# A prepass with its four Q/K pairs first and its four V rounds behind them, and its staging moved into bytes of the loop's tiles

## The chip, the cores and the metric

The kernel runs on one core of a Trainium2 chip. The time is the device time of one execution in microseconds (us). Before the change it was 1764.0, 1775.37 and 1770.44 us in three runs, median 1770.44. The profile comes from one further execution of the same program, 1772.28 us, whose profiled span is 1770.6 us.

Engines are named as in the profile: PE is TensorE (matrix multiplications; PEld its loads of stationary operands), DVE is VectorE, ACT is ScalarE, POOL is GpSimd, SP is SyncE. SP and ACT issue nearly all DMAs; the queue of a DMA is named after its issuer (SPq, ACTq). A DMA that waits at the head of an engine's queue holds whatever that engine was to do next.

## What is computed

Two attentions of the same 2048 x 640 input are mixed by a gate per token. One is a local attention with 8 taps at a distance of two tokens (32 heads of 20). The other walks through 64 segments of 32 tokens and carries 8 memory rows from segment to segment (32 heads of 192):

```python
mem = mem0
for s in range(n_seg):                      # 64 segments, one after the other
    h = concat([mem, x[s * 32:(s + 1) * 32]])          # 40 rows
    q, k, v = h @ Wq, h @ Wk, h @ Wv                   # 640 -> 32 heads x 192
    p = softmax(where(mask, q @ k.T * scale, -1e9))
    o = (p @ v) @ Wo                                   # back to 640
    mem = o[:8]
    outs.append(o[8:])
a = concat(outs)
out = sigmoid(x @ gate_w) * a + (1 - sigmoid(x @ gate_w)) * b     # b: the local attention
```

A segment needs the memory of the one before, so the loop over segments can't be spread out. What depends on x alone can be computed ahead of it.

## The kernel before

The program has four stages.

**Part B** (`part_b`) is the local attention. On its way it prepares the other stages: `make_xT(b)` transposes 512 tokens of x at a time, POOL copies them into `xh_blk` (L184, L185), and SP stores that for the loop's segments (L186). POOL makes a second copy of each segment's last eight tokens, `zx_blk` (L190), which SP stores as well (L191, 160 KB each, four of them). Late in part B, SP loads all of that back as `zT` (640 KB, L320), and POOL makes a second layout of it, `zTi` (L321). `zT` has token `i` of segment `s` at column `s i`, `zTi` at column `i s`. Both are 128 x 2560 bf16. `load_early` issues the first weight slices once the first xh store has been issued, then 20 copies of Wo slices into a scratch in DRAM (`wscr`).

**The weights** are 80 slices of 128 x 1536 bf16 (384 KB): 20 each of Wq, Wk, Wv and 20 of Wo (12 `oa`, 8 `ob`). 14 of them are streamed anew in every segment through five buffers (`wst`); 66 stay resident. The resident ones are sorted in the order of their use (`use`, L374) and loaded on SP in four lots: 21 early ones in part B, 24 when part B ends (`load_late(0)`), 8 in the last Q/K pair (`load_late(1)`, N_MID), and 13 behind the prepass (`load_late(2)`, N_LAST), so those 13 stand ahead of the loop's own streaming on SP's queue.

**The prepass** (`prepass`) projects the last eight tokens of all 64 segments, 512 columns, with Wq, Wk and Wv. `project_qk(p)` is a pair: two groups of eight heads of Wq (p = 0, 1) or of Wk (p = 2, 3), 24 groups of five matmuls of 128 x 512, whose results ACT and DVE evict in turn (`evac`, L75 and L77) into a tile ZS of 128 x 64 x 192. ACT then stores ZS to `zpk_dram`, in two DMAs. `project_v(R)` is a V round: four steps of three groups of five matmuls, evicted into a tile ZV, which ACT stores with two DMAs for each step. All groups take their PSUM from one pool of eight banks. The order is pair 0, V 0, pair 1, V 1, pair 2, V 2, pair 3, V 3.

**The loop** (`part_a`) runs 64 segments in an order written out by hand for PE, ACT and DVE. Per segment it multiplies 32 columns (`hT`) with all of Wq and Wk (`m_qk`, L568), then Wv (`m_v`, L661) and Wo (`o_group`, L725). It reads the segment's part of `zpk_dram` (`load_z`, L543, and `load_vz`, L548; ACT's queue). Behind it, `part_z` computes the output rows of the last eight tokens of each segment.

The scheduler of the framework decides which PSUM bank a group gets and which semaphore a wait goes to; the order of the instructions within each engine follows the program above, except where `issue_after` ties an instruction to a DMA.

```python
for s0, s1 in ((0, 8), (8, nseg)):
    nc.scalar.dma_start(self.zpk_dram[s0:s1, :, z0:z0 + 192].rearrange("s p f -> p s f"), ZS[:, s0:s1, :])
```

Of the kernel before, what the change touches and what calls it, by code (L numbers as in the profile page):

```python
# [10 lines left out]
BF = mybir.dt.bfloat16  # L11
# [3 lines left out]
N_STREAM = 14  # L15
N_EARLY = 21
N_MID = 8
ZVB = 4
N_LAST = 13
WBUFS = 5  # L20
# [6 lines left out]
class _K:  # L27

    def __init__(self, ctx, tc, A_x, A_mem0, A_Wq, A_Wk, A_Wv, A_Wo, seg_len, B_wqkv, B_wo, gate_w, out):
        self.ctx, self.tc, self.nc = ctx, tc, tc.nc  # L30
        self.x2d = A_x.rearrange("b s d -> (b s) d")
        self.out2d = out.rearrange("b s d -> (b s) d")
        self.mem0 = A_mem0.rearrange("b m d -> (b m) d")
        self.Wq = A_Wq.rearrange("d h e -> d (h e)")
        self.Wk = A_Wk.rearrange("d h e -> d (h e)")
        self.Wv = A_Wv.rearrange("d h e -> d (h e)")
        self.Wo = A_Wo.rearrange("h e d -> (h e) d")
        self.wqkv, self.wo, self.gate_w = B_wqkv, B_wo, gate_w
# [12 lines left out]
        self.hTp = ctx.enter_context(tc.tile_pool(name="hTp", bufs=2))  # L51
        self.zctx = ExitStack()
        self._evac_i = 0
        self.evac_pat = _DEV.get("evac_pat", "aaad")
# [33 lines left out]
    def part_b(self):  # L88

        nc, tc, KC, S = self.nc, self.tc, self.KC, self.S  # L90
        NQ, HALO = 121, 14
        BQ = 4 * NQ
        scale_b = 20.0 ** (-0.5)
        self.bsc_dram = self.dram.tile([S, 640], BF, name="bsc_dram")
        self.zT_dram = self.dram.tile([128, KC, S // 32, 8], BF, name="zT_dram")
        self.oz_dram = self.dram.tile([S // 32, 128, 384], BF, name="oz_dram")
# [4 lines left out]
        with ExitStack() as ctx:  # L101
# [56 lines left out]
            def make_xT(b):  # L158
                t0 = 512 * b
                for kc in range(KC):  # L160
                    ps = bank(BF, "ps_xT")
# [26 lines left out]
                self.first_store = self.first_store or xh_store.ins  # L188
                zx = blkp.tile([128, KC, 16, 8], BF, name="zx_blk")
                nc.gpsimd.tensor_copy(zx[:].rearrange("p c s i -> p s c i"), xv[:, :, :, 24:32])  # L190
                nc.sync.dma_start(self.zT_dram[:, :, 16 * b:16 * b + 16, :].rearrange("p c s i -> p c (s i)"),  # L191
                                  zx[:].rearrange("p c s i -> p c (s i)"))

# [7 lines left out]
            def make_v(b):  # L201
                nq, nu, c0 = shape_of(b)
                nk = nq + 7
                for u in range(nu):
                    V = wk.tile([128, 652], BF, name=f"bV{u}")
                    nc.gpsimd.memset(V[:, 640:652], 0.0)
                    k0 = c0 + 242 * (u // 2) + u % 2
# [81 lines left out]
            nc.scalar.preload_act_table_set("natural_log_exp_and_others")  # L289
            zp = self.zctx.enter_context(tc.tile_pool(name="pre_z", bufs=1, side="right"))  # L290
            self.zT = zp.tile([128, KC, S // 4], BF, name="zT")
            self.zTi = zp.tile([128, KC, S // 4], BF, name="zTi")
            sel_ones = wp.tile([128, 160], BF, name="sel_ones")
            steps = [(b, g) for b in range((S + BQ - 1) // BQ) for g in range(8)]
            self.first_store = None
# [6 lines left out]
            for i, (b, g) in enumerate(steps):  # L302
# [11 lines left out]
                if (b, g) == (1, 4):  # L314
                    self.build_sel(self.const, sel_ones[:])
                    self.hT0 = self.load_seg(0)
                    for kc in range(KC):
                        nc.sync.dma_start(self.hT0[:, kc, 0:8], self.mem0[:, kc * 128:(kc + 1) * 128].rearrange("m p -> p m"))
                if (b, g) == (S // 512 - 1, 2):
                    nc.sync.dma_start(self.zT[:], self.zT_dram[:].rearrange("p c s i -> p c (s i)"))  # L320
                    nc.gpsimd.tensor_copy(self.zTi[:].rearrange("p c (i s) -> p c i s", i=8),  # L321
                                          self.zT[:].rearrange("p c (s i) -> p c i s", i=8))
                if g == 6 and i + 8 < len(steps):
# [32 lines left out]
    def weights_setup(self):  # L356
# [13 lines left out]
        rest = [k for k in keys if k not in self.stream_keys]  # L370
        use = [g for p in range(4) for g in (("qqkk"[p], 2 * (p % 2)), ("qqkk"[p], 2 * (p % 2) + 1), ("v", p))]
        rest.sort(key=lambda k: use.index(k[:2]) if k[:2] in use else 99)
        n = (0, N_EARLY, len(rest) - N_MID - N_LAST, len(rest) - N_LAST, len(rest))
        self.early, *self.late = [rest[n[x]:n[x + 1]] for x in range(4)]  # L374
        self.wres = self.ctx.enter_context(tc.tile_pool(name="wres", bufs=1))
# [43 lines left out]
    def prepass(self):  # L419
# [6 lines left out]
        def project_qk(p, pool):  # L426
# [3 lines left out]
            if p == 3:  # L430
                self.load_late(1)
            for r in range(2):
# [12 lines left out]

        def project_v(R):
            sls = [self.get_slice(("v", R, kc)) for kc in range(KC)]
            for st in range(NZ // 128):
# [68 lines left out]
    def part_a(self):  # L517
# [4 lines left out]
        with ctx:  # L522
            pers = ctx.enter_context(tc.tile_pool(name="a_pers", bufs=1, reuse_waits="tile"))
            ZQ = pers.tile([128, 224 + 768 + 1152], BF, name="ZQ")
            Vz = ZQ[:, 224:608]
            QTa = ZQ[:, 992:2144].rearrange("p (b r c i) -> p b r c i", b=6, r=2, i=8)
            Es = [ZQ[:, 608 * h:608 * h + 224].rearrange("p (a f) -> p a f", a=2) for h in range(2)]
            zst = ZQ[:, 32:416]
            oTz = zst.rearrange("p (c q) -> p c q", q=8)
            whi = ZQ[:, 1376:1376 + 640]  # L530
            KV = pers.tile([128, 1536], BF, name="KV")
# [3 lines left out]
            a4 = pers.tile([128, 160], BF, name="a4")  # L535
            KTz = pers.tile([128, 12, 32], BF, name="KTz")

# [4 lines left out]
            def load_z(s):  # L542
                nc.scalar.dma_start(ZQ[:, 608:1376], self.zpk_dram[s, :, 384:1152])  # L543
                nc.gpsimd.tensor_copy(KTz[:].rearrange("p c (R i) -> p c R i", i=8),  # L544
                                      ZQ[:, 608:992].rearrange("p (R c i) -> p c R i", c=12, i=8))

# [342 lines left out]
def kernel(  # L889
# [57 lines left out]
```

## Time and profile before

| | us |
|---|---|
| median of three runs (lowest, highest) | 1770.44 (1764.0, 1775.37) |
| the profiled execution | 1772.28 |
| its span | 1770.6 |
| part B | 0 to 232.0 |
| prepass, first to last matmul | 232.03 to 389.3 |
| segment 0 of the loop | 389.3 to 428.6 |
| segment 1 | 428.6 to 448.8 |

Busy shares of the whole span: PE 95% (1675.4 us), ACT 49%, DVE 37%, POOL 4%. The DMA engines move 467.81 MB, 264 GB/s on average. In the slices of the page, each a fortieth of the span (44.3 us), the ones of part B and the prepass look like this (a digit is the busy share in tenths):

```profile
PE   6888999987999999999999999999999999999989
ACT  3766632223555555555555555555555555555550
DMA  5951176579999999899999989989989999998991
```

PE is near full from the fifth slice to the end but for the ninth and tenth, 354 to 443 us, where the prepass ends and the loop starts. ACT and DVE carry part B; in the loop PE does. An idle engine costs time only where another one waits for it, so what counts is PE's idle time, and the clock at which it runs.

### The profile page before, as it was taken

Reading aid. Unit: us, or ns where it says so; the run is one execution under the profiler, and the core shown is the slowest. Engines: PE = TensorE matmul, PEld = TensorE weight load, DVE = VectorE, ACT = ScalarE, POOL = GpSimd, SP = SyncE. Lnnn points to the kernel's source line nnn. Section 1 sums busy time; section 2 is a strip of 40 time slices with the busy share of each in tenths; the row PEclk is TensorE's granted clock in tenths of the full one; section 3 lists DMA queues with packets and bytes.
Section 4 is the critical chain, followed back from the end, with each engine's and each line's share of the span. In section 5 each row is a group of like instructions: output and inputs, shape, how many; then the busy total and the mean of one; then the engine's idle time right before and its main releaser. Section 6 shows DMA issues by size and latency. Waiting matters only on the chain.

```text
span 1770.6 us, 82392 instructions
## 1 busy us (share of the span) xinstructions
PE 1675.4 (95%) x36512; PEld 995.8 (56%) x36527; DVE 651.8 (37%) x2047; ACT 869.2 (49%) x2377; POOL 75.0 (4%) x151
## 2 busy tenths in 40 slices
PE   6888999987999999999999999999999999999989
PEld 3555544434565655556555555555555555555557
DVE  4565532322333333333333333333333333333330
ACT  3766632223555555555555555555555555555550
POOL 6011000000000000000000000000000000000000
PEclk9999999998999999999999999999999999999999
DMA  5951176579999999899999989989989999998991
GB/s 161 331 128 50 38 258 164 154 234 328 290 303 303 303 301 306 297 297 311 302 298 303 306 284 304 302 289 297 304 297 298 301 298 303 303 296 292 306 299 30
DMA packets 283480, 467.81 MB, mean 264 GB/s; under 512 B 97524, under 2 KB 158452, under 8 KB 283124
## 3 DMA queue, kind: packets, MB, share of 16 engines
q1 hardware_dynamic: 181400, 403.14, 68.9%
q10 hardware_dynamic: 101724, 59.41, 11.6%
q8 instruction: 285, 4.67, 1.1%
q14 instruction: 71, 0.58, 0.1%
HBM read 428.13 MB, written 42.20 MB: 266 GB/s over the span
## 4 chain that ended last, share of the span: by engine, by line
PE 83%; ACT 6%; DMA 6%; issue 3%; DVE 1%; ACTq 0%; SPq 0%; POOL 0%; DVEq 0%; POOLq 0%
PE ps_qk L568 25%; PE ps_v L661 13%; PE ps_wo L725 11%; PE ps_qkT L585 6%; PE ps_S L615 5%; PE ps_pre L438 5%; PE ps_oT L684 3%; PE ps_z L879 3%; PE ps_bqk L224 3%; ACT bP L247 2%; PE ps_pre L453 2%; ACT ZQ L806 2%; PE ps_bv L211 1%; PE ps_mem L735 1%; PE ps_S L624 1%
## 5 line engine op out<-in xcount | busy, mean ns | idle before, releaser
L577 ACT CAST KV<-ps_qk 128x384 bf16<-128x384 f32 x448 | 208.5, 480 | 333.0 <-PE ps_qk L568 185.0
L568 PEld LDWEIGHTS <-hT 128*32 128x32 bf16 x10240 | 247.7, 96 | 154.5 <-DVE hT L738 12.8
L568 PE MATMUL ps_qk<-wlate_k,hT 128*32 128x384 bf16 x4352 | 269.9, 329 | 1.2 <-issue 0.9
L592 DVE COPY ZQ<-ps_qkT 128x384 bf16<-128x384 bf16 x256 | 91.6, 358 | 390.0 <-PE ps_qkT L585 220.3
L568 PE MATMUL ps_qk<-wres_q,hT 128*32 128x384 bf16 x4096 | 227.4, 329 | 4.6 <-ACT ZV L75 3.8
L633 ACT ACTIVATE ZQ<-ps_S 32x224 bf16<-32x224 f32 x512 | 178.1, 348 | 44.3 <-PE ps_S L624 39.8
L725 PEld LDWEIGHTS <-KV 128*32 128x32 bf16 x6144 | 154.1, 96 | 67.7 <-issue 20.2
L661 PE MATMUL ps_v<-wlate_v,hT 128*32 128x384 bf16 x2816 | 160.6, 329 | 0.0
L568 PE MATMUL ps_qk<-wst,hT 128*32 128x384 bf16 x1792 | 153.9, 329 | 1.0 <-issue 1.0
L661 PEld LDWEIGHTS <-hT 128*32 128x32 bf16 x5120 | 113.4, 96 | 72.7 <-issue 10.0
L725 PE MATMUL ps_wo<-wlate_oa,KV 128*32 128x384 bf16 x2560 | 140.5, 327 | 2.9 <-issue 2.8
L615 PE MATMUL ps_S<-ZQ,KV 128*128 128x160 bf16 (+1 forms) x1024 | 136.9, 238 | 3.3 <-DMA ZQ<-zpk_dram 3.3
L585 PE MATMUL ps_qkT<-ident,KV 128*128 128x128 bf16 x1536 | 130.7, 221 | 0.4 <-issue 0.3
L725 PE MATMUL ps_wo<-wlate_ob,KV 128*32 128x256 bf16 x2688 | 123.6, 275 | 7.3 <-issue 7.3
L585 PEld LDWEIGHTS <-KV 128*128 128x128 bf16 x1536 | 89.4, 98 | 61.9 <-issue 40.9
L695 DVE CAST KV<-ps_oT 128x192 bf16<-128x192 f32 x256 | 79.4, 351 | 64.8 <-PE ps_oT L689 64.8
L615 PEld LDWEIGHTS <-KV 128*128 128x128 bf16 (+1 forms) x1024 | 59.1, 95 | 72.6 <-issue 45.3
L695 ACT CAST KV<-ps_oT 128x192 bf16<-128x192 f32 x256 | 69.6, 326 | 59.0 <-PE ps_oT L689 59.0
L544 POOL COPY KTz<-ZQ 128x384 bf16<-128x384 bf16 x64 | 32.6, 509 | 1492.1 <-DMA ZQ<-zpk_dram 850.6
L661 PE MATMUL ps_v<-wst,hT 128*32 128x384 bf16 x1024 | 87.1, 330 | 9.1 <-DMA wst<-in_A_Wv_dram 9.1
L738 DVE CAST hT<-ps_mem 128x24 bf16<-128x24 f32 x126 | 22.6, 179 | 197.4 <-PE ps_mem L735 197.4
L668 ACT CAST KV<-ps_v 128x384 bf16<-128x384 f32 x192 | 92.4, 481 | 3.1
(127 smaller groups left out, 2316.8 us busy)
## 6 DMA issues: line engine op xcount, KB each, us to landing
wst<-in_A_Wq_dram SPq DMA_DIRECT2D x260, 384.0 KB
wst<-in_A_Wv_dram SPq DMA_DIRECT2D x260, 384.0 KB
wst<-in_A_Wk_dram SPq DMA_DIRECT2D x195, 384.0 KB
wst<-wscr SPq DMA_DIRECT2D x192, 384.0 KB
ZQ<-zpk_dram ACTq DMA_DIRECT2D x64, 192.0 KB
zpk_dram<-ZS ACTq DMA_DIRECT2D x4, 2688.0 KB
wscr<-in_A_Wo_dram SPq DMA_DIRECT2D x20, 384.0 KB
wlate_k<-in_A_Wk_dram SPq DMA_DIRECT2D x17, 384.0 KB
```

Source lines behind the costliest of these rows:

```text
L224: nc.tensor.matmul(ps[:, 0:nn], lhsT=wqk[n][:, kc, 4 * g:4 * g + 4, :].rearrange("p h d -> p (h d)"), rhs=xT[:, kc, o0:o0 + nn], start=(kc ...
L438: nc.tensor.matmul(ps[:], lhsT=sls[r][kc][:, c0:c0 + 128], rhs=zT[:, kc, :], start=(kc == 0), stop=(kc == KC - 1))
L568: nc.tensor.matmul(pq[32 * j:32 * j + 32, 0:384], lhsT=hT[:, kc, :], rhs=sl[:, 384 * j:384 * j + 384], start=(kc == 0), stop=(kc == KC - 1 ...
L577: cp(sts[i], pqs[i][:, 0:384])
L585: nc.tensor.transpose(pT[:, t, :, :, :].rearrange("p j b i -> p (j b i)"), st[:, 128 * t:128 * t + 128], self.ident[:])
L592: nc.vector.tensor_copy(q_blocks(R)[:, 1:5, :, :].rearrange("p b c i -> p c b i"), pT.rearrange("p t j b i -> p (t j) b i"))
L615: nc.tensor.matmul(grid(h, par)[:, :, 0:80].rearrange("p j (b r i) -> p j b r i", r=2, i=8)[:, :, :, r, :], lhsT=KT[k0:k1, 12 * r + c:12 * ...
L633: nc.scalar.activation(E[ps], pSs[h][ps, :, 112 * j:112 * j + 112], ACT.Exp, scale=scale_a)
L661: nc.tensor.matmul(pvs[R][32 * j:32 * j + 32, 0:384], lhsT=hT[:, kc, :], rhs=sl[:, 384 * j:384 * j + 384], start=(kc == 0), stop=(kc == KC ...
L668: cp(V[R], pvs[R][:, 0:384])
L695: cps[j % 2](oTxs[2 * h + j // 2][:, 6 * (j % 2):6 * (j % 2) + 6, :], pos[j][:, 0:240].rearrange("p (c q) -> p c q", q=40)[:, :, 8:40])
L725: nc.tensor.matmul(pso[part][32 * jj:32 * jj + 32, 0:n], lhsT=oTxs[2 * (R // 2) + j // 2][:, 6 * (j % 2) + 3 * (R % 2) + t, :], rhs=o_weig ...
```

## The change

- The prepass runs the four Q/K pairs first, then the four V rounds. The weights are sorted and loaded in that order (q, k, v).
- There is one x^T of the last tokens, `zTi` in the layout `i s`, in a tile `TZ` of the constants. POOL writes it straight from the transposed x in `make_xT`, after the xh store is issued. `zx_blk`, the DRAM tensor `zT_dram`, its four stores, its load and the copy at L321 are gone. The pairs now multiply with `zTi` too, so their evictions read PSUM with the eight tokens of one segment 64 elements apart.
- Each ZS goes out in one DMA of 64 segments instead of two (8 and 56).
- ZV lies in the bytes of pair 2's ZS, and eight late slices (N_V) are loaded into the bytes of pair 3's, issued ahead of the V rounds. The lots are now 23 early, 27 at the end of part B, 4 in the last pair, 8 ahead of the V rounds and 4 (N_LAST) behind the prepass.
- In the loop, KV, KTz, Vz, the output staging and one E tile lie in the bytes of `TZ`; the rest of ZQ is a tile `ZB` that also holds `a4`.
- The selection masks (`build_sel`) are built in the last `make_xT` instead of at step (1, 4), and the memsets of V's padding go from POOL to DVE.

```diff
-N_EARLY = 21
-N_MID = 8
+N_EARLY = 23
+N_MID = 4
+N_V = 8
+N_LAST = 4
 ZVB = 4
-N_LAST = 13
...
+        self.TZ = self.const.tile([128, self.KC * self.S // 4], BF, name="TZ")
+        self.zTi = self.TZ[:].rearrange("p (c x) -> p c x", c=self.KC)
...
-                zx = blkp.tile([128, KC, 16, 8], BF, name="zx_blk")
-                nc.gpsimd.tensor_copy(zx[:].rearrange("p c s i -> p s c i"), xv[:, :, :, 24:32])
-                nc.sync.dma_start(self.zT_dram[:, :, 16 * b:16 * b + 16, :].rearrange("p c s i -> p c (s i)"),
-                                  zx[:].rearrange("p c s i -> p c (s i)"))
+                with tc.issue_after(xh_store.ins):
+                    nc.gpsimd.tensor_copy(zTi[:, :, :, 16 * b:16 * b + 16],
+                                          xv[:, :, :, 24:32].rearrange("p s c i -> p c i s"))
+                    if b == 3:
+                        self.build_sel(self.const, sel_ones[:])
...
-                    nc.gpsimd.memset(V[:, 640:652], 0.0)
+                    nc.vector.memset(V[:, 640:652], 0.0)
...
-                if (b, g) == (S // 512 - 1, 2):
-                    nc.sync.dma_start(self.zT[:], self.zT_dram[:].rearrange("p c s i -> p c (s i)"))
-                    nc.gpsimd.tensor_copy(self.zTi[:].rearrange("p c (i s) -> p c i s", i=8),
-                                          self.zT[:].rearrange("p c (s i) -> p c i s", i=8))
...
-        use = [g for p in range(4) for g in (("qqkk"[p], 2 * (p % 2)), ("qqkk"[p], 2 * (p % 2) + 1), ("v", p))]
+        use = [(m, R) for m in "qkv" for R in range(4)]
...
-                            nc.tensor.matmul(ps[:], lhsT=sls[r][kc][:, c0:c0 + 128], rhs=zT[:, kc, :],
+                            nc.tensor.matmul(ps[:], lhsT=sls[r][kc][:, c0:c0 + 128], rhs=zTi[:, kc, :],
...
-                        self.evac(ZS[:, :, zc:zc + 8], ps[:].rearrange("p (s i) -> p s i", i=8))
-            z0 = 768 + 192 * (1 - Rp) if m == "q" else 384 + 192 * Rp
-            for s0, s1 in ((0, 8), (8, nseg)):
-                nc.scalar.dma_start(self.zpk_dram[s0:s1, :, z0:z0 + 192].rearrange("s p f -> p s f"), ZS[:, s0:s1, :])
+                        self.evac(ZS[:, :, zc:zc + 8], ps[:].rearrange("p (i s) -> p s i", i=8))
+            nc.scalar.dma_start(self.zpk_dram[:, :, z0:z0 + 192].rearrange("s p f -> p s f"), ZS[:])
...
-        with tc.tile_pool(name="pre_zv", bufs=ZVB, side="right", reuse_waits="tile") as zvp, \
-                tc.tile_pool(name="pre_zs1", bufs=1, side="right", reuse_waits="tile") as zs1:
-            zT, zTi = self.zT, self.zTi
+        zTi = self.zTi
+        with tc.tile_pool(name="pre_zs1", bufs=1, side="right", reuse_waits="tile") as zs1:
             with tc.tile_pool(name="pre_zs0", bufs=1, reuse_waits="tile") as zs0:
                 project_qk(0, zs0)
-                project_v(0)
                 project_qk(1, zs1)
-                project_v(1)
                 project_qk(2, zs0)
-            project_v(2)
             project_qk(3, zs1)
-            project_v(3)
-        self.zctx.close()
+        vs = [[self.get_slice(("v", R, kc)) for kc in range(KC)] for R in range(4)]
+        self.load_late(2, "right")
+        with tc.tile_pool(name="pre_zv", bufs=ZVB, reuse_waits="tile") as zvp:
+            for R in range(4):
+                project_v(vs[R], R)
...
-            ZQ = pers.tile([128, 224 + 768 + 1152], BF, name="ZQ")
+            ZB = pers.tile([128, 1536 + 160], BF, name="ZB")
+            KV, ZA = self.TZ[:, 0:1536], self.TZ[:, 1920:2528]
...
-    k.load_late(2)
+    k.load_late(3)
```

More of the change, by code (lines that the diff above doesn't have):

```diff
@@ L51, in __init__ @@
         self.hTp = ctx.enter_context(tc.tile_pool(name="hTp", bufs=2))
-        self.zctx = ExitStack()
+        self.TZ = self.const.tile([128, self.KC * self.S // 4], BF, name="TZ")
+        self.zTi = self.TZ[:].rearrange("p (c x) -> p c x", c=self.KC)
         self._evac_i = 0
@@ L94, in part_b @@
         self.bsc_dram = self.dram.tile([S, 640], BF, name="bsc_dram")
-        self.zT_dram = self.dram.tile([128, KC, S // 32, 8], BF, name="zT_dram")
         self.oz_dram = self.dram.tile([S // 32, 128, 384], BF, name="oz_dram")
@@ L289, in part_b @@
             nc.scalar.preload_act_table_set("natural_log_exp_and_others")
-            zp = self.zctx.enter_context(tc.tile_pool(name="pre_z", bufs=1, side="right"))
-            self.zT = zp.tile([128, KC, S // 4], BF, name="zT")
-            self.zTi = zp.tile([128, KC, S // 4], BF, name="zTi")
+            steps = [(b, g) for b in range((S + BQ - 1) // BQ) for g in range(8)]
+            zTi = self.zTi.rearrange("p c (i s) -> p c i s", i=8)
             sel_ones = wp.tile([128, 160], BF, name="sel_ones")
-            steps = [(b, g) for b in range((S + BQ - 1) // BQ) for g in range(8)]
             self.first_store = None
@@ L314, in part_b @@
                 if (b, g) == (1, 4):
-                    self.build_sel(self.const, sel_ones[:])
                     self.hT0 = self.load_seg(0)
@@ L370, in weights_setup @@
         rest = [k for k in keys if k not in self.stream_keys]
-        use = [g for p in range(4) for g in (("qqkk"[p], 2 * (p % 2)), ("qqkk"[p], 2 * (p % 2) + 1), ("v", p))]
+        use = [(m, R) for m in "qkv" for R in range(4)]
         rest.sort(key=lambda k: use.index(k[:2]) if k[:2] in use else 99)
-        n = (0, N_EARLY, len(rest) - N_MID - N_LAST, len(rest) - N_LAST, len(rest))
-        self.early, *self.late = [rest[n[x]:n[x + 1]] for x in range(4)]
+        n = (0, N_EARLY, -N_MID - N_V - N_LAST, -N_V - N_LAST, -N_LAST, None)
+        self.early, *self.late = [rest[n[x]:n[x + 1]] for x in range(5)]
         self.wres = self.ctx.enter_context(tc.tile_pool(name="wres", bufs=1))
@@ L431, in project_qk @@
                 self.load_late(1)
+            z0 = 768 + 192 * (1 - Rp) if m == "q" else 384 + 192 * Rp
             for r in range(2):
@@ L437, in project_qk, with project_v @@
                         for kc in range(KC):
-                            nc.tensor.matmul(ps[:], lhsT=sls[r][kc][:, c0:c0 + 128], rhs=zT[:, kc, :],
+                            nc.tensor.matmul(ps[:], lhsT=sls[r][kc][:, c0:c0 + 128], rhs=zTi[:, kc, :],
                                              start=(kc == 0), stop=(kc == KC - 1))
                         zc = 96 * r + 8 * (4 * t + j)
-                        self.evac(ZS[:, :, zc:zc + 8], ps[:].rearrange("p (s i) -> p s i", i=8))
-            z0 = 768 + 192 * (1 - Rp) if m == "q" else 384 + 192 * Rp
-            for s0, s1 in ((0, 8), (8, nseg)):
-                nc.scalar.dma_start(self.zpk_dram[s0:s1, :, z0:z0 + 192].rearrange("s p f -> p s f"), ZS[:, s0:s1, :])
-        def project_v(R):
-            sls = [self.get_slice(("v", R, kc)) for kc in range(KC)]
+                        self.evac(ZS[:, :, zc:zc + 8], ps[:].rearrange("p (i s) -> p s i", i=8))
+            nc.scalar.dma_start(self.zpk_dram[:, :, z0:z0 + 192].rearrange("s p f -> p s f"), ZS[:])
+        def project_v(sls, R):
             for st in range(NZ // 128):
@@ L523, in part_a @@
             pers = ctx.enter_context(tc.tile_pool(name="a_pers", bufs=1, reuse_waits="tile"))
-            ZQ = pers.tile([128, 224 + 768 + 1152], BF, name="ZQ")
[L525 to L528, printed above, removed]
+            ZB = pers.tile([128, 1536 + 160], BF, name="ZB")
+            KV, ZA = self.TZ[:, 0:1536], self.TZ[:, 1920:2528]
+            Vz = ZA[:, 224:608]
+            QTa = ZB[:, 384:1536].rearrange("p (b r c i) -> p b r c i", b=6, r=2, i=8)
+            Es = [z[:, 0:224].rearrange("p (a f) -> p a f", a=2) for z in (ZA, ZB)]
+            zst = ZA[:, 32:416]
             oTz = zst.rearrange("p (c q) -> p c q", q=8)
-            whi = ZQ[:, 1376:1376 + 640]
-            KV = pers.tile([128, 1536], BF, name="KV")
+            whi = ZB[:, 768:768 + 640]
             KT = KV[:, 0:768].rearrange("p (c k) -> p c k", k=32)
@@ L534, in part_a @@
             oTxs = [v.rearrange("p (c q) -> p c q", q=32) for v in V]
-            a4 = pers.tile([128, 160], BF, name="a4")
-            KTz = pers.tile([128, 12, 32], BF, name="KTz")
+            a4 = ZB[:, 1536:1696]
+            KTz = self.TZ[:, 1536:1920].rearrange("p (c k) -> p c k", k=32)
             psm = ctx.enter_context(tc.tile_pool(name="psm", bufs=2, space=bass.MemoryType.PSUM, reuse_waits="tile"))
@@ L542, in load_z @@
             def load_z(s):
-                nc.scalar.dma_start(ZQ[:, 608:1376], self.zpk_dram[s, :, 384:1152])
+                nc.scalar.dma_start(ZB[:, 0:768], self.zpk_dram[s, :, 384:1152])
                 nc.gpsimd.tensor_copy(KTz[:].rearrange("p c (R i) -> p c R i", i=8),
-                                      ZQ[:, 608:992].rearrange("p (R c i) -> p c R i", c=12, i=8))
+                                      ZB[:, 0:384].rearrange("p (R c i) -> p c R i", c=12, i=8))
             def load_vz(s):
```

## The prediction

> **What bounds the kernel now.** I read the page first (TensorE busy 95% of the span, so only its stalls and clock can be won), then the busy times by stage, because the change reorders one stage, the prepass, and so moves what stands before and after it.
>
> ```profile
> core 0: us, PE busy (x) PEld busy (x) DVE busy (x) ACT busy (x) POOL busy (x), PEclk, DMA share, GB/s
> 0.00:232.00 232.00, 197.76 (x2724) 115.43 (x2725) 126.65 (x233) 139.46 (x249) 42.42 (x87) 0.96 0.46 136
> 271.00:389.30 118.30, 116.37 (x530) 52.59 (x538) 36.69 (x55) 29.71 (x54) 0.00 (x0) 1.00 0.62 173
> 389.30:428.60 39.30, 25.13 (x491) 14.39 (x490) 7.95 (x27) 11.79 (x34) 0.51 (x1) 0.83 0.95 323
> 428.60:448.80 20.20, 19.96 (x501) 12.04 (x502) 7.30 (x27) 10.60 (x32) 0.51 (x1) 1.00 0.93 301
> ```
> Columns: window, its length, busy us and count per engine, granted clock, DMA share, GB/s. Part B ends at 232.0. In the prepass TensorE is nearly full. Segment 0 takes 39.3 us where segment 1 takes 20.2: 19.1 us too many, at a clock of 0.83. That is nearly all there is to win. Its chain of waits (start, us, what):
>
> ```profile
> 388.78 3.79 DMA wst<-in_A_Wk_dram
> 392.57 0.09 ACT ZV L75
> ...
> 409.13 7.79 DMA wst<-in_A_Wv_dram
> ```
> and its instructions in order of time (start, us, engine, line, operation; in brackets the idle time before):
>
> ```profile
> 397.45 6.71 SPq L399 DMA_DIRECT2D wlate_oa<-wscr  x6
> ...
> 403.21 0.47 PE L615 MATMUL ps_S<-ZQ,KV 128*128 128x160 bf16 x4 [2.33 <-DMA ZQ<-zpk_dram]
> ...
> 404.20 4.40 SPq L399 DMA_DIRECT2D wlate_ob<-wscr  x7
> ...
> 404.81 1.50 PE L568 MATMUL ps_qk<-wres_q,hT 128*32 128x384 bf16 x16
> ...
> 416.96 0.51 PE L661 MATMUL ps_v<-wst,hT 128*32 128x384 bf16 x4 [7.42 <-DMA wst<-in_A_Wv_dram]
> ```
> Three stalls (3.79, 2.33, 7.42 us) and a small one (0.31): 13.85 us. The rest, 19.1 - 13.85 = 5.2, is slow clock: the 16 matmuls at 404.81 take 1.50 us, the same 16 at 399.38 took 0.82. The 7.42 us stall is a queue: 13 late slices stand ahead of one slice of Wv on SP. The first two come from ScalarE, which also issues the Z stores:
>
> ```profile
> L75 ACT CAST ZS<-ps_pre x48: 586/586/641, 233.3 to 375.4; 128x512 bf16<-128x512 f32 x48
> ...
>   DMA zpk_dram<-ZV: 25.9, 3
> ...
> 382.82 9.63 ACTq L460 DMA_DIRECT2D zpk_dram<-ZV  x4
> 392.55 1.56 ACT L75 CAST ZV<-ps_pre 128x512 bf16<-128x512 f32 x3 [9.22 <-DMA wst<-in_A_Wk_dram]
> ```
> After each pair's ZS store (landing 13.45 us after its issue) the next V stores hold ScalarE's queue 8.9 to 9.6 us, and evictions queue behind them. The last round has the loop behind it, not another pair: hence 3.79 at 389.
>
> **The change, part by part.** The profiled execution took 1772.28 us (span 1770.6); the median of three is 1770.44, 1.84 below it.
>
> *Matmuls of the prepass: the same.* Before, a pair's 120 matmuls end 25.9 us after they began (232.03 to 257.92), a V round's 60 take 12.95. Four of each are 155.4; the stage took 157.3 (232.03 to 389.32). So 1.9 us of stalls go, the largest 1.04 at 360.
>
> *Pairs back to back.* A group of five 128x512 matmuls takes 1.08 us; its eviction starts 0.42 us after the next group begins and lasts 0.59 (ScalarE) or 0.69 (VectorE), so a bank is free 1.1 us after its group's end. In the built program before, each of these groups takes a bank used six groups or more earlier. In the new one, four groups early in each of pairs 1, 2 and 3 wait for VectorE's eviction of the group 4, 3, 2 and 1 earlier. Distances 4 and 3 are covered (two groups are 2.16 us); distance 1 costs 1.1, distance 2 about 0.1: 3 x 1.2 = **+3.6 us**, at least 0 if the eviction drains ahead, at most 6. The 1.04 us stall at 360 left the clock at 1.00 (window 360 to 380), so I add nothing for it.
>
> *Strided eviction.* x^T lies with the segment inside, so 96 evictions read PSUM with a step of 64 elements. No row of before reads PSUM so. The nearest: VectorE's eviction that permutes runs of eight takes 0.36 us, as the contiguous one does; POOL's zTi copy, reading single elements, takes 4.83/2560 = 1.89 ns an element against 0.717/640 = 1.12 for runs of eight, factor 1.7. Two engines alternate, so each has 2.16 us an eviction; 0.69 x 1.7 = 1.17 fits, and only the three distance-1 waits grow, by 0.5 each. I take 0 (nearest engine and memory), range 0 to +1.5.
>
> [...]
>
> *V rounds.* The ScalarE block happens once, behind pair 3, not four times. In V0 its stores hold ScalarE until the ZS store has landed, and the next ones wait for DMA semaphores held by the first of eight late slices, issued only when ZS has landed (1.2 + 13.45 = 14.7 us after pair 3's end). Before, at 350.95, the same knot took until 360.54, 9.6 us, plus an eviction of 0.6: ScalarE is through at 24.9, where TensorE wants that bank 21 groups after pair 3, at 22.7: **+2.2 us** (0 to 4, with a clock drop at the upper end). V1 to V3 run free. Removing 1.9 and adding 3.6 + 2.2 makes the prepass **+3.9 us**.
>
> *Segment 0.* V3's evictions are no longer blocked: the first groups wait only for VectorE's last ones, 0.4 us; the Z loads are issued a round early, so the 2.33 goes; load_vz behind V3's stores costs up to 0.5. On SP four late slices stand ahead of the Wv slice, not 13. Before, the streamed slice ahead of them was issued 3.76 us after the first loop matmul (393.19 to 396.95) and 15 tiles landed in 20.0 us, 1.33 each (0.98 at the 402 GB/s of 410 to 420). That one, four and Wv's are six tiles, 5.9 to 8.0 us: landing 9.7 to 11.8 after the start, with up to 1.3 of latency on top, wanted at 10.5 (as in segment 1) plus the 0.9 just named: a stall of 0 to 1.5, taken 0.7. A stall of over 2 us costs 5.2/3 = 1.7 us of clock besides; I take a third of that. Segment 0: 20.2 + 0.4 + 0.5 + 0.7 + 0.6 = 22.4 against 39.3: **-16.9 us**. The nine late slices that left the loop's start are hidden under 104 us of pairs and 52 of V rounds (DMA share there 0.62); without that cover each costs 1.33.
>
> *Part B and other queues.* SP loses four zT stores and the 640 KB load; POOL loses the 4.83 us copy, its four 0.72 copies become strided (1.2 by the factor), and its 18 memsets of 0.1 go to VectorE (55% busy there). The masks are built at the last x^T block. The early loads start up to 4.5 us sooner (POOL waits that long for the band before the zx copy that SP follows), but are two more slices, of 28.4/21 = 1.35 each (29.62 to 58). TensorE waits here for ScalarE and VectorE, so I take **0**, from -2 to +2. The zT path ended in a 9.9 us POOL wait that nothing else waited for.
>
> *The loop.* The built program's instructions and waits in a steady segment are the same ones; only addresses differ. 0, with a tail: 0.05 us a segment is 3.2 us.
>
> Sum: +3.9 - 16.9 + 0 = -13.0: 1759.3 against the profiled execution, and 1770.44 - 13.0 = 1757.4 against the median, said as **1758 us**.
>
> **The rivals.**
> 1. *Everything hidden.* Semaphore waits and late loads land in time: the 3.6, 2.2 and segment 0's 2.2 shrink to 2 in all: -1.9 - 19.1 + 2 = -19, 1751 us. For: the DMA queues have slack in the pairs. Against: a distance-1 wait can't be hidden. Chance 0.2.
> 2. *The loop's start stays choked.* Loads that no longer queue there still share the DMA engines with V3's stores and the streaming (301 GB/s in segment 1): the Wv slice lands as late as before, 7.4 + 1.7 us stay. For: DMA share 0.95 in segment 0 already. Against: nine slices fewer at 1.33 are 12 us less. -13.0 + 9.1 - 1.3 (0.7 and 0.6 counted already) = -5, 1765 us. Chance 0.17.
> 3. *Slower: the eviction sets the pace of the pairs.* In 96 groups TensorE needs an eviction each 1.08 us from two engines. From a strided eviction of 2.16 us (factor 3.1 on 0.69) on, pairs run at eviction speed; the gain is eaten where a group takes 13.0/96 = 0.14 more, at 2.43 us (factor 3.5). At factor 4.2 an eviction takes 2.9 us, a group 1.45: 0.37 x 96 = +36, less 13.0: +23, 1793 us. For: no row shows the pattern. Against: the 1.7 of POOL. Chance 0.1.
> 4. *Part B or the prepass loses what the loop gains*, through part B's queues or loads of late slices colliding with ZS stores: about +10, so -3, 1767 us. Chance 0.13.
>
> [...]
>
> **How the numbers follow.** The forecast has 0.4, the rivals 0.2, 0.17, 0.1 and 0.13. A measurement of this kernel can tell about 1%, 17.7 us, from no change: faster means below 1752.7, slower above 1788.2. Faster: three quarters of rival 1 and a quarter of the forecast's own spread (its unknowns of -2, -3.6, -2.2 and the runs' spread of 11 us): 0.15 + 0.1 = 0.25. Slower: rival 3 and a little of 4: 0.11. Same: 0.64. The range goes from 1746 (rival 1 with part B's 2 and the runs' lower side) to 1774 (rival 4 with the runs' upper side); it leaves out rival 3 and the tails.
>
> **What would show it.** Segment 0 near 22 us with no stall at the Wv slice; ZV evictions blocked once, not four times; three stalls of 1.1 us a group or two into pairs 1, 2, 3; 0.6 to 0.7 us per strided eviction. Wrong if evictions pass 2.2 us, if the pairs' clock falls below 0.95, or if steady segments differ from 20.2 us.

## The result and the profile after

| | before | changed |
|---|---|---|
| median of 12 runs, us (lowest, highest) | 1772.34 (1764.0, 1777.08) | 1762.45 (1757.04, 1772.14) |
| ratio to before, 95% interval | | 0.995 (0.9929 to 0.9971) |
| span of the profiled execution, us | 1770.6 | 1759.7 |

The changed kernel is 0.5% faster: 9 us by the ratio, between 5 and 13, within the 1% that was called no change. The busy times by stage of the changed kernel (window, length, busy us and count per engine, clock, DMA share, GB/s):

```profile
254.80:281.00 26.20, 25.31 (x117) 11.44 (x118) 8.30 (x12) 6.78 (x12) 0.00 (x0) 1.00 0.59 165
334.60:391.20 56.60, 54.28 (x239) 24.05 (x242) 15.50 (x24) 12.96 (x25) 0.51 (x1) 0.97 0.84 245
391.20:416.08 24.88, 19.90 (x492) 12.02 (x495) 7.91 (x27) 10.66 (x32) 0.00 (x0) 1.00 0.94 304
```

The first row is the second pair, the second row the V rounds, the third segment 0. Segment 0 now takes 24.9 us at full clock, not 39.3 at 0.83; the second pair keeps a clock of 1.00. The V rounds (334.6 to 391.2) have a clock of 0.97: there is a new loss there. TensorE's waits of the changed kernel from 225 to 480 us (total us, times, longest):

```profile
PE ps_pre L434 <- DVE ZS L79: 2.3, 3, 0.8
PE ps_qkT L577 <- ACT TZ L569: 2.2, 1, 2.2
PE ps_pre L446 <- ACT ZV L77: 2.1, 1, 2.1
PE ps_v L653 <- DMA wst<-in_A_Wv_dram: 2.0, 1, 2.0
```

These four groups are nearly all that is left: three waits of a group for the eviction of the group just before it (distance 1, as the prediction calls them) in the pairs, one wait in V1, and two at the loop's start. The V1 wait and what follows it, in order of time:

```profile
360.31 4.44 PE L446 MATMUL ps_pre<-wlate_v,TZ 128*128 128x512 bf16 x12 [2.06 <-ACT ZV L77]
...
365.23 2.75 PE L446 MATMUL ps_pre<-wlate_v,TZ 128*128 128x512 bf16 x11
```

Twelve matmuls take 4.44 us there, and eleven take 2.75 five microseconds later: some 1.7 us go to a slow clock behind a stall of 2.06.

To compare many kernels I use two stretches of each profile: from the first matmul of pair 0 to the loop's first matmul ("prepass"), and from there to the start of segment 0's tail update on VectorE, early in segment 1 ("start"). The new order, the stores and the late loads act in their sum; what the change does to part B lies outside it. The column of part B is the time at which it ends. The ratios below compare each kernel with runs of the kernel before on the same chip; the stages come from one profile each, and the two profiles of the changed kernel differ by 0.9 us in the prepass and 0.7 in the start.

| kernel | part B | prepass | start | sum |
|---|---|---|---|---|
| before | 232.03 | 161.16 | 37.19 | 198.35 |
| before, second profile | 227.01 | 162.12 | 37.06 | 199.18 |
| changed | 228.82 | 162.40 | 26.23 | 188.63 |
| changed, second profile | 228.42 | 161.48 | 26.94 | 188.42 |
| order only | 228.55 | 159.40 | 34.98 | 194.38 |
| eight late slices back | 227.95 | 159.36 | 36.22 | 195.58 |
| late slices behind V0 | 228.11 | 162.50 | 25.27 | 187.77 |
| banks in turn | 226.82 | 165.61 | 27.27 | 192.88 |
| ZS of pair 3 from SP | 227.24 | 158.46 | 27.06 | 185.52 |
| load_vz later | 226.64 | 163.18 | 28.44 | 191.62 |
| first Wv slice ahead | 225.11 | 161.47 | 25.47 | 186.94 |
| banks in turn, pairs only | 225.94 | 158.36 | 25.90 | 184.26 |
| three edits | 226.88 | 155.99 | 25.02 | 181.01 |
| four edits | 226.58 | 156.45 | 26.10 | 182.55 |

The rest of the loop, whose instructions are the same everywhere, took 1247.8 to 1267.6 us for segments 1 to 62 in these profiles, with 19.7 us for the quickest segments in both the kernel before and the changed one. That spread of 20 us is larger than any edit's effect, so a total shows less than a stage does.

### The profile page after: what moved, and what is told of

It is laid out like the page before. It is cut to its first block, busy times and chain, and to the rows that moved or that the text cites. A ratio compares the mean times of both kernels' runs of the same rounds, so it can differ in the third digit from the quotient of the medians.

```text
span 1759.7 us, 82388 instructions
## 1 busy us (share of the span) xinstructions
PE 1675.3 (95%) x36512; PEld 998.3 (57%) x36527; DVE 651.0 (37%) x2065; ACT 872.1 (50%) x2377; POOL 71.3 (4%) x132
## 4 chain that ended last, share of the span: by engine, by line
PE 85%; ACT 6%; DMA 3%; issue 2%; DVE 2%; ACTq 0%; SPq 0%; DVEq 0%
PE ps_qk L560 25%; PE ps_v L653 13%; PE ps_wo L717 12%; PE ps_qkT L577 6%; PE ps_pre L434 6%; PE ps_S L607 5%; PE ps_oT L676 3%; PE ps_z L871 3%; PE ps_bqk L226 3%; ACT bP L249 2%; PE ps_pre L446 2%; ACT ZB L798 2%; PE ps_mem L727 1%; PE ps_bv L213 1%; PE ps_S L616 1%
## 5 line engine op out<-in xcount | busy, mean ns | idle before, releaser
L569 ACT CAST TZ<-ps_qk 128x384 bf16<-128x384 f32 x448 | 208.8, 481 | 332.3 <-PE ps_qk L560 185.5
L584 DVE COPY ZB<-ps_qkT 128x384 bf16<-128x384 bf16 x256 | 91.6, 358 | 377.6 <-PE ps_qkT L577 212.3
L717 PEld LDWEIGHTS <-TZ 128*32 128x32 bf16 x6144 | 154.6, 96 | 65.3 <-issue 17.4
L560 PE MATMUL ps_qk<-wlate_k,hT 128*32 128x384 bf16 x2560 | 159.8, 328 | 0.1
L717 PE MATMUL ps_wo<-wlate_oa,TZ 128*32 128x384 bf16 x2560 | 140.8, 328 | 3.5 <-issue 3.4
L607 PE MATMUL ps_S<-ZB,TZ 128*128 128x160 bf16 (+1 forms) x1024 | 136.5, 237 | 0.8 <-issue 0.8
L577 PE MATMUL ps_qkT<-ident,TZ 128*128 128x128 bf16 x1536 | 130.2, 220 | 3.0 <-ACT TZ L569 2.2
L717 PE MATMUL ps_wo<-wlate_ob,TZ 128*32 128x256 bf16 x2688 | 124.5, 276 | 5.9 <-issue 5.9
L560 PE MATMUL ps_qk<-wres_k,hT 128*32 128x384 bf16 x1792 | 119.8, 328 | 1.5 <-issue 1.1
L660 ACT CAST TZ<-ps_v 128x384 bf16<-128x384 f32 x192 | 92.7, 483 | 3.1
```

Of the source, the lines that this page charges most:

```text
L560: nc.tensor.matmul(pq[32 * j:32 * j + 32, 0:384], lhsT=hT[:, kc, :], rhs=sl[:, 384 * j:384 * j + 384], start=(kc == 0), stop=(kc == KC - 1 ...
L569: cp(sts[i], pqs[i][:, 0:384])
L577: nc.tensor.transpose(pT[:, t, :, :, :].rearrange("p j b i -> p (j b i)"), st[:, 128 * t:128 * t + 128], self.ident[:])
L584: nc.vector.tensor_copy(q_blocks(R)[:, 1:5, :, :].rearrange("p b c i -> p c b i"), pT.rearrange("p t j b i -> p (t j) b i"))
L607: nc.tensor.matmul(grid(h, par)[:, :, 0:80].rearrange("p j (b r i) -> p j b r i", r=2, i=8)[:, :, :, r, :], lhsT=KT[k0:k1, 12 * r + c:12 * ...
L660: cp(V[R], pvs[R][:, 0:384])
```

## The experiments

**Order alone.** The kernel before, with pairs first and the weights sorted to match; 13 late slices stay behind the prepass.

```diff
-                project_v(0)
                 project_qk(1, zs1)
-                project_v(1)
                 project_qk(2, zs0)
-            project_v(2)
             project_qk(3, zs1)
-            project_v(3)
+            for R in range(4):
+                project_v(R)
```

> The kernel before with one thing changed: the order of the prepass (four pairs, then four V rounds, weights sorted q, k, v); 13 late slices still stand behind it on SP. If the two halves of the change add up (order: 3.79 + 2.33 + 0.31 us of stalls and some 3 us of slow clock go; lots: 7.42 + 1.7), this one is about 8 us faster than before. Rival: SP's queue sets when the Wv slice lands, 23.8 us after the loop's first matmul as before, so what ScalarE no longer delays is waited for at the Wv slice instead. Then the stall there grows from 7.4 to about 12 us, only the 3.79 ahead of the loop and 1.9 in the prepass are won, three distance-1 waits cost 2.3, and the sum is about -3 us.

Measured: ratio to before 0.9983 (0.9957 to 1.001), the two stretches 4.0 us shorter than before's first profile. TensorE's waits of this kernel, same window:

```profile
PE ps_v L659 <- DMA wst<-in_A_Wv_dram: 9.4, 1, 9.4
PE ps_qkT L583 <- ACT KV L575: 2.7, 2, 2.5
PE ps_pre L438 <- DVE ZS L77: 2.3, 3, 0.8
```

The three distance-1 waits come with the order, before any other part of the change. The wait for Wv grew from 7.4 to 9.4 us and ended 24.1 us after the loop's first matmul (387.95 to 412.07), as in the kernel before (23.8). Freeing ScalarE moved TensorE's wait to SP's queue. The rival's mechanism holds, though it put the longer wait at 12 us: the two halves don't add up.

**Late slices back at the loop's start.** The changed kernel with `N_V = 0` and `N_LAST = 12`.

> The changed kernel with N_V = 0 and N_LAST = 12: the eight slices that it loads ahead of the V rounds are issued behind the prepass again. Theory (SP's queue sets the loop's start): 14 tiles ahead instead of 6, the Wv slice lands 6 to 10 us later, stall there 8 to 12 us and 1.7 of slow clock; V1's stall of 2.1 us and the slow clock behind it go, as no late slice holds ScalarE's stores. Total +3 to +7 us against the changed kernel, -3 to -8 against before. Rival (the lots do not matter, the order does): the Wv stall stays near 2 us, and the kernel is some 4 us faster than the changed one.

Measured: 0.9979 (0.9958 to 0.9999), the sum 7 us longer than the changed kernel's. Of the waits, these two decide:

```profile
PE ps_v L653 <- DMA wst<-in_A_Wv_dram: 10.8, 1, 10.8
PE ps_pre L446 <- ACT ZV L77: 0.8, 1, 0.8
```

The Wv wait is 10.8 us instead of 2.0, and the one in V1 0.8 instead of 2.1: the eight slices cost 3.0 us in the prepass and save 10.0 at the loop's start. So the order is worth 4 us of the change and the late slices, with it, some 6 to 7. (This kernel has all of the change but the lots, and its sum is 1.2 us above that of the order alone: the other parts together win nothing that single profiles could show.)

**Late slices issued behind V0.** The loads were moved one call later in the program:

```diff
-        self.load_late(2, "right")
+        late2 = self.load_late(2, "right", now=False)
...
                 project_v(vs[R], R)
+                if R == 0:
+                    late2()
```

> The changed kernel with the eight late slices issued behind V round 0 instead of ahead of it, so that ScalarE's third and fourth store of V0 do not wait for semaphores that these loads hold. Theory: the 2.1 us stall in V1 goes and the half-speed matmuls behind it (1.8 us): -3.9 us, if the loads still land before the loop. Rival: the ZS store alone keeps ScalarE until then, the stall stays within 0.5 us of 2.1.

Measured: 0.9953 (0.9924 to 0.9982), V1's stall 2.11 us. It tells nothing on the theory: the edit did not move the loads. SP issues them 15.3 us after V0's first matmul with and without it, and ScalarE's second hold in V0 and V1 is 4.05 us instead of 4.33. It serves as one more profile of the changed kernel.

**Eight banks in turn.**

```diff
-        t = self.psum.tile([128, tot], dtype, tag="ps", name=name)
+        self._bank = (getattr(self, "_bank", -1) + 1) % 8
+        t = self.psum.tile([128, tot], dtype, tag=f"ps{self._bank}", name=name)
```

> The changed kernel with the eight PSUM banks of the prepass named one by one and used in turn. In the built program no group then waits for an eviction less than four groups back. Theory: the three stalls of 0.78 us at the start of pairs 1, 2 and 3 go, pairs take 25.9 us each, -2.3 us. Rival: the strided evictions are late anyway and the stalls come back elsewhere: 0.

Measured: 0.9957 (0.9938 to 0.9975); the prepass is 3.2 us longer. Its waits:

```profile
PE ps_pre L447 <- ACT ZV L78: 7.5, 2, 6.2
```

No wait for an eviction is left in the pairs. They take 103.6 us instead of 106.4, so the three waits had cost 2.8 us, 0.94 each: 0.78 of idle time, and the rest because a group that waits can't overlap the end of the one before: in the profile matmuls begin 0.216 us apart and last 0.38 each, an overlap of 0.16. But the V rounds take 6.0 us more. Both waits are for ScalarE's evictions, and in V0 ScalarE stands at its stores for 11.9 us (338.23) and evicts nothing until 350.17. In the changed kernel it stands there for 9.11, and TensorE does not wait in V0. The likely reason, which no row shows directly: a fixed turn soon asks for a bank that only ScalarE can free, where free choice keeps going with the banks that VectorE frees.

**The fourth pair's ZS stored by SP.**

```diff
-            nc.scalar.dma_start(self.zpk_dram[:, :, z0:z0 + 192].rearrange("s p f -> p s f"), ZS[:])
+            (nc.sync if p == 3 else nc.scalar).dma_start(
+                self.zpk_dram[:, :, z0:z0 + 192].rearrange("s p f -> p s f"), ZS[:])
```

> The changed kernel with the fourth pair's ZS store issued by SP instead of ScalarE; SP has only the eight late slices behind it, and they wait for that store anyway. Theory: ScalarE is held in V0 and V1 because its own DMA queue is full of that 3.1 MB store. Then its stores of V0 go out at once (under 1 us each for two instead of 9.1 us for four), the 2.1 us stall in V1 and the slow clock behind it go: the prepass takes about 158.5 us instead of 162.4, -3.9 us. Rival: the stores wait for semaphores that the late slices hold, whoever stores ZS; then ScalarE is free again as late as now and the stall stays near 2 us.

Measured: 0.9905 (0.9873 to 0.9936), prepass 158.46 us: the 3.9 us are gone. ScalarE's DMA issues in V0 in the changed kernel (start, us, queue, line):

```profile
336.21 0.37 ACTq L438 DMA_DIRECT2D zpk_dram<-ZS  x1
...
341.76 9.11 ACTq L453 DMA_DIRECT2D zpk_dram<-ZV  x4
350.92 1.57 ACT L77 CAST ZV<-ps_pre 128x512 bf16<-128x512 f32 x3 [8.63 <-issue]
355.23 4.33 ACTq L453 DMA_DIRECT2D zpk_dram<-ZV  x4
359.67 1.57 ACT L77 CAST ZV<-ps_pre 128x512 bf16<-128x512 f32 x3 [7.19 <-DMA wlate_ob<-wscr]
```

and with ZS on SP's queue:

```profile
334.62 0.37 SPq L438 DMA_DIRECT2D zpk_dram<-ZS  x1
...
337.77 1.94 ACTq L453 DMA_DIRECT2D zpk_dram<-ZV  x2
...
341.27 2.27 ACTq L453 DMA_DIRECT2D zpk_dram<-ZV  x2
...
348.22 6.93 ACTq L453 DMA_DIRECT2D zpk_dram<-ZV  x2
```

Four stores took 9.11 us behind ZS on one queue, two pairs of them 1.94 and 2.27 us beside it. There is still one hold of 6.93 us at 348.22; TensorE does not wait for it. The store's place in ScalarE's queue is one half of the cause. The late slices are the other: the stall in V1 follows the second hold (4.33 us), and in it two of ScalarE's stores go out at 356.56 and 359.04, just as late slices land whose semaphores they use (356.55 and 359.02). Without late slices there (second experiment) the first hold stays, and the stall is 0.8 us. This edit also sends the slices later (from 354.63 instead of 350.50), so it does not part the two. Of the 3.9 us, 0.8 come back at the loop's start, where the wait at load_vz is 3.1 us instead of 2.2.

**load_vz later.** Segment 0's load goes behind the eviction of its fourth Q/K group.

```diff
             load_z(0)
-            load_vz(0)
...
                     store()
-                    load_vz(s)
+                load_vz(s)
```

> The changed kernel with segment 0's load_vz moved on ScalarE's queue behind the eviction of its fourth Q/K group, where the other segments have it. Theory: the 2.2 us stall at the third transpose of segment 0 is ScalarE standing at load_vz until V3's stores have landed. It goes: from the loop's first matmul to the mark of segment 1 some 24 us instead of 26.2. Rival: the Wv slice lands at a set time (14.7 us after the loop's start), so its stall grows from 2.0 to about 4 us and nothing is won.

Measured: 0.9958 (0.9932 to 0.9983), start 28.44 us, 2.2 longer. The wait at the transpose is gone (0.2 us left), and this stands in its place:

```profile
404.50 0.51 PE L652 MATMUL ps_v<-wst,hT 128*32 128x384 bf16 x4 [3.94 <-DMA wst<-in_A_Wv_dram]
406.39 1.47 PE L652 MATMUL ps_v<-wlate_v,hT 128*32 128x384 bf16 x16
```

The Wv slice came 14.7 us after the loop's first matmul (389.83), just as in the changed kernel (391.22 to 405.95). TensorE merely waited longer, and behind the longer stall the clock fell too: 16 matmuls take 1.47 us, not 0.83. The rival holds.

**The first Wv slice ahead of the four.**

```diff
                 m_v(0)
+                if s == 0:
+                    with tc.issue_after(self.last_load.ins):
+                        self.late_issue()
```

> The changed kernel with its last four late slices issued behind segment 0's first streamed Wv slice instead of ahead of it. Theory (SP's order): that slice lands 4 tiles earlier, its 2.0 us stall goes, -2.0 us at the loop's start. Rival: the next Wv slices now stand behind the four and stall instead, by the same 2 us; total 0.

Measured: 0.9915 (0.9887 to 0.9944); start 25.47, 0.8 less than in the changed kernel's first profile and 1.5 less than in its second. The first slice is not waited for any more; a later one, now behind the four, is, for 1.2 us. Between the two theories, and not far above the spread of the profiles.

**Banks in turn in the pairs alone.**

```diff
+        self._bank = (getattr(self, "_bank", -1) + 1) % 8
+        t = self.psum.tile([128, tot], dtype, tag=f"ps{self._bank}" if self.turn else "ps", name=name)
...
+            with tc.tile_pool(name="psum_v", bufs=8, space=bass.MemoryType.PSUM, reuse_waits="tile") as self.psum:
+                self.turn = False
```

> The changed kernel with the banks taken in turn in the four pairs only; the V rounds choose freely again from a pool of their own. Theory: the three stalls of 0.78 us are gone as with banks in turn everywhere (-2.3 us), and the V rounds' stall returns from 7.5 to about 2.1 us, so the prepass takes about 160 us instead of 162.4. Rival: the V rounds stall as with banks in turn everywhere, because the state of the banks at pair 3's end decides; prepass about 165.6 us.

Measured: 0.9916 (0.9883 to 0.9949), prepass 158.36: 4.0 us less. The pairs are free of waits, and V1's stall is 1.5 us, not followed by a slow clock (12 matmuls in 2.81 us). The 4.0 are 2.8 of the pairs (103.6 us instead of 106.4) and 1.2 of the V rounds, where the stall is 0.5 shorter and the slow clock behind it (4.44 - 2.81 = 1.6) is gone, but 0.5 goes to a wait for VectorE. The rival is out.

**The kernel before, a second profile.**

> The kernel before, unchanged, profiled a second time. Question: are the 3.2 us by which part B was shorter in the changed kernel's profile the change's? Theory: only in part: the clock dip of 2.4 us that before's profile shows at 206 to 213 us is not the program's and is absent here, while VectorE again stands for some 2.5 us during POOL's 4.83 us copy. Part B then ends at 225 to 230 us. Rival: part B ends at 231 to 233 us again, so the change did shorten it.

Measured: part B ends at 227.0 us, earlier than in the changed kernel (228.8). So the 3.2 us by which part B differs in the first two profiles can't be put down to the change: two profiles of one kernel differ by 5.0. Of the details, one was expected wrongly: a clock dip is there again, at another place (0.79 from 198 to 206 us, after 0.57 from 206 to 214 in the first profile). Two of VectorE's mask products took 2.57 us during POOL's copy, as expected.

**The changed kernel again, and two versions with several edits,** on one chip.

> The changed kernel, unchanged, a second time, as the measure for the runs beside it. Prepass to the loop's first matmul 162 to 163.5 us, from there to segment 1's mark 25 to 27 us, as the five kernels with the same staging had; ratio to before 0.995 again. If prepass or loop start differ by over 1 us from the first profile, single profiles cannot tell the 1 to 2 us effects.

> The changed kernel with three of the edits together: pair 3's ZS stored by SP, the first Wv slice ahead of the four late ones, banks in turn in the pairs. If the terms are separate: -3.9, -0.8 and -2.3 (the edit on the banks gave -4.0 in the prepass, of which some 1.8 is V1's, counted once): prepass 156 to 156.5 us, loop start 25 to 27 us, about -6 us against the changed kernel, ratio to before 0.991. Rival: ScalarE free earlier only moves the wait to load_vz (3.1 us in the run with SP's store), loop start 27 us or more.

> The same with segment 0's load_vz moved behind the fourth eviction too. Alone this edit only moved the wait to the Wv slice (stall 3.9 us). With that slice now four tiles earlier the theory expects neither stall: loop start 23 to 24.5 us, prepass 156 to 156.5 us, about -8 us against the changed kernel, ratio to before 0.990. Rival: the Wv slice still lands 13 to 14 us after the loop's start, and the loop start stays at 25 us or more.

Measured: the changed kernel's prepass is 161.48 us, half a microsecond below what was expected, and its start 26.94. Both are within 1 us of the first profile, the bound that was set. Ratios: changed 0.9936 (0.991 to 0.9961), three edits 0.9893 (0.9864 to 0.9921), four edits 0.9907 (0.9884 to 0.9929). The prepass of the three edits is 155.99 us, against 155.4 for its matmuls alone. Its start is 25.02 us: the wait at load_vz remains (2.2), the one at Wv is 0.2. With load_vz later as well, TensorE waits 1.8 us for a slice of Wv and 1.3 us for an eviction of ScalarE. The rival holds: the start is 26.1 us.

The sum is no shorter. The version with three edits, with the shortest stretches, beats both kernels; its interval just meets that of the changed kernel, so the gain over it rests on the stages: 188.4 to 188.6 against 181.0 us.

## Why the prediction was right, point by point

The forecast was -13.0 us and within 1%; the stages gave 198.35 - 188.63 = -9.7, by the second profiles -10.8, and the runs about -9. The direction, the place and most of the mechanisms held; the gain was put a quarter to a third too high. The prepass, from its first to its last matmul, became 5.1 us longer (157.4 to 162.5), not 3.9, and segment 0 14.4 us shorter, not 16.9. "Within 1%" was an easy mark, as any gain below 17.7 us lies inside it: the stages test the mechanisms, the verdict hardly does. Of the signs that the prediction named, no stall at the Wv slice and segment 0 near 22 us did not come. The terms of the sum, as sized and as measured in the changed kernel's first profile:

| step | predicted | measured |
|---|---|---|
| stalls of the old prepass that go | -1.9 | -2.0 (157.36 - 155.4) |
| three distance-1 waits | +3.6 | +2.8 (2.3 of it idle) |
| strided eviction | 0 | 0 |
| V1 behind late slices and ZS | +2.2 | +2.1 and 1.7 of clock |
| segment 0 | 22.4 us | 24.9 us |
| of it, load_vz | 0.5 | 2.2 |
| of it, the Wv slice | 0.7 | 2.0 |
| part B | 0 (-2 to +2) | not told apart from the spread of 5 us |

- *Stalls of the old prepass.* Their sum was right. The largest is 1.23 us and ends at 361.17; the 1.04 us that the prediction gives for it is an idle time of ScalarE near it.
- *Distance-1 waits.* 1.2 us each was too much by 0.26, and the misreading is one of a single matmul. An eviction was taken to start 0.42 us after the next group begins. In the rows it starts 0.42 us after the last matmul of its own group begins, which is 0.20 after the next group would begin, as matmuls begin 0.216 us apart. The chain of waits of the changed kernel:

```profile
261.62 8.38 PE ps_pre L434 x38
270.02 0.70 DVE ZS L79
270.77 2.54 PE ps_pre L434 x11
```

The last matmul before the wait begins at 269.61. The next would begin at 269.82 and begins at 270.77.

- *Strided eviction.* With a step of 64 elements the mean is 587 ns on ScalarE and 692 on VectorE, as contiguous (591 and 692 in the kernel before). Rival 3 is out.
- *V1.* The stall was right to 0.2 us, and so was its cause in two parts, the ZS store and the late slices behind it: it shrinks to 0.8 without the slices there, and goes with the store on SP's queue. The clock stood only at the upper end of that term's range, and it was nearly as dear as the stall.
- *load_vz.* This is one of the two worst-sized terms, beside V1's clock. It had been charged with 0.5 us for standing behind V3's stores. What it waits for is their landing: ScalarE has finished its third eviction at 395.27, V3's last store lands at 397.95, and load_vz goes out at 398.13.
- *The Wv slice.* It landed 14.7 us after the loop's first matmul, where 9.7 to 13.1 was said, the last 1.3 of it an allowance of the author's for latency. The four late slices alone took 5.99 us to issue and the slice 5.5 to land:

```profile
394.37 5.99 SPq L394 DMA_DIRECT2D wlate_ob<-wscr  x4
...
398.13 0.34 ACTq L540 DMA_DIRECT2D TZ<-zpk_dram  x1
```

  The prediction priced the tiles on SP's queue at the rate at which they land, and left out a wait: of the 5.99 us, SP stands 2.9 (395.15 to 398.03) between the first and the second slice. It waits there for the same semaphore as load_vz, that of V3's last store (397.95). The two also go out 0.1 us apart, just behind that landing, in the runs with ZS from SP, with load_vz later and with three edits. So the waits for load_vz and for the Wv slice both hang on the landing of V3's stores. That the stall was only 2.0 is due to load_vz, which held TensorE until then.
- *Rival 2* (a choked start) was partly right: less queue, but a set landing time. Experiments one and six show that the waits at the loop's start stand behind one another, so that removing an early one lengthens the last. The 16.9 us of expected gain there became 14.4 (39.3 to 24.9) because load_vz cost 1.7 us more than its term and the Wv slice 1.3 more, while the 0.6 set aside for a slow clock was not needed.
- *Rival 1* needed the distance-1 waits to be hidden; they were not.

Whether fewer DMAs in V3 would bring the Wv slice earlier was not tried.

## What to carry to other kernels

Where several waits follow one another at a stage's start, find the one whose end is fixed by a queue: it takes back what is won ahead of it (with load_vz later, its 2.2 us went and the wait for the Wv slice grew from 2.0 to 3.9). When you price a queue, look for waits between its entries too, not only for the rate at which they land (here 2.9 of 5.99 us). A large store belongs in a queue where nothing urgent stands behind it, and moving one store from ScalarE to SP was worth as much in the prepass here as the banks (3.9 and 4.0 us). A buffer choice that removes waits in one stage can add more in the next (banks in turn: 2.8 us less in the pairs, 6.0 more in the V rounds), so judge it by both.

## What the runs showed of the hardware

- *Stalls near 2 us and the clock.* In V1, stalls of 2.06, 2.11 and 2.29 us were followed by twelve matmuls in 4.4 to 4.5 us, stalls of 1.97, 1.86 and 1.54 by the same in 2.81. At the loop's start, where twelve matmuls take 1.08 us, stalls of 2.22 and 3.30 us (the changed kernel, banks in turn) left no such mark, and stalls of 2.13 and 3.09 (banks in turn in the pairs, ZS from SP) were followed by 1.76 and 1.61. So in these runs the length of a stall did not decide alone; what else did is not shown.
- *VectorE's products of two tiles during POOL's copy.* In the kernel before, VectorE's two mask products (0.67 us each elsewhere) took 3.76 us during POOL's 4.83 us copy:

```profile
142.13 4.83 POOL L321 COPY zTi<-zT 128x2560 bf16<-128x2560 bf16 x1 [9.89 <-DMA zT<-zT_dram]
...
144.30 3.76 DVE L251 TENSOR_TENSOR bP<-bP,band 128x968 bf16<-128x968 bf16 x2 [1.88 <-ACT bP L247]
```

In all three profiles with the copy, the first of the two products ends 0.5 us after the copy does, and the second takes its usual 0.65. An eviction that VectorE made during the copy took 0.66 us, as elsewhere (139.22 in the second profile of the kernel before).

The change removes that copy. Between two operations of ScalarE around it, three profiles of programs with the copy have 7.58, 6.40 and 7.96 us, the eleven profiles without it 6.16 to 6.18 (the bkT evictions at 142.81 and 150.40 in the first): 0.2 to 1.8 us were won there, which the prediction had at nothing.
- *Part B's clock dips come and go.* Between 36 and 48 us seven of the eleven profiles with the changed part B show a clock of 0.86, the others 1.00; the two profiles of the changed kernel itself are one of each (0.86 and 1.00), and the same stretch of work takes 7.97 and 6.41 us in them. By 50 us most of that is made up, and part B ends 0.4 us apart. So this dip does not explain why part B ends between 225.1 and 228.8 us in the eleven; that stays open. A difference of 1.5 us in part B between two single profiles thus says nothing on the change.
